# The first feature steps as a written list of single operations, up to step 28, and the second w_in block loaded ahead of x

## The chip, the cores and the metric

One NeuronCore of a Trainium2 chip runs the whole program. The metric is the device time of one execution in microseconds (us), and the figure given for a kernel is the median of its runs. Five engines work beside each other, each through its own queue in order: TensorE (PE in the profile, its weight loads are PEld), VectorE (DVE), ScalarE (ACT), GpSimd (POOL) and SyncE (SP), which here issues nearly all transfers (DMA). TensorE writes its results to PSUM, a memory of banks from which VectorE and ScalarE read them.

## The reference, cut to what matters

```python
# x [8,8,512,64], state [8,8,32,64], scale = 1/8
scores = scale * x @ state^T                 # [8,8,512,32]
a  = softmax(scores);   xread = a  @ state   # read by tokens
a2 = softmax(scale * state @ x^T); sread = a2 @ x   # read by slots
t  = concat([xread, sread], axis=2)          # 544 rows a batch, 4352 in all
t  = t.transpose(0,2,1,3).reshape(4352, 512)
# first block: w_in [512,2048], w_out [2048,512]
h = t @ w_in;  g = max(h, 0)**2;  t = g @ w_out
# second block: w_in [512,1024], g_ln [1024], w_out [1024,512]
h = t @ w_in;  s = h * softmax(h)
out = (s - mean(s)) / sqrt(var(s) + 1e-6) * g_ln @ w_out
```

The weight matrices reach the chip in 64-bit floats, and the kernel makes 32-bit numbers of them itself.

## The kernel before, in words

**Precision.** Every product that has to be exact is made of three matmuls. A number is split into a high part, which ScalarE writes by a copy to the matmul's format, and a low part, which VectorE writes by subtracting the high part. `triple` (lines 147 to 149) then adds high times high, high times low and low times high in one PSUM bank. Each of these matmuls has 512 columns.

**The tokens' read is never formed.** For a batch the product state @ w_in is made first (`ps_sw`, in 512-feature columns, called a chunk), and the hidden layer is the softmax `a` times that product. One **feature step** is one batch and 128 of the 2048 hidden features: six matmuls into `ps_h` (two contraction halves of three), ScalarE's relu and the square, the split of the square into `gh` (ScalarE) and `gl` (VectorE, line 830), and twelve matmuls `acc<-gh/gl,w1out` that add the step to four banks of output. There are 16 steps to a batch and 144 in all: eight batches, and a ninth block that holds all `sread` rows. The list `items` gives their order; the first 32 steps go chunk by chunk between batches 0 and 1, and steps 0 to 15 are their chunks 0 and 1.

**Weights are made ready beside that.** `convert_parts` turns a 128x512 block of 64-bit words into a high and a low part: on VectorE `cz`, `cu` twice, `ch`, `cz` and the low part (lines 215, 220, 221, 225, 231, 232), on ScalarE the exponent `cz` (line 216) between VectorE's first `cz` and its `ch`, and the high part (line 228) after `ch`. Sixteen blocks of w_in (`i0` to `if`, written to `w1i_d` and used for `ps_sw`) and sixteen of w_out (`o0` to `of`) go through it. `sw_part` makes `ps_sw` for two batches a call, ScalarE copies it to `ev_sw` (line 328) and it goes to DRAM (`sw_d`), from where `load_sw` fetches a batch's chunk into `stg` (line 406) and it is split again (`sw`).

**What sets the order.** The scheduler is switched off for four engines (`manual_schedule`): each engine runs its instructions in the order in which the code makes them. For the steps 0 to 15 this order is a written list, `PLAN`, of names such as `T02` (transpose x of batch 0, head pair 2), `i0` (the next piece of w_in block 0), `H00` (hidden of batch 0, feature 0), `G`, `L` (high, low), `P001` (one of four projections), `X0` (load x of batch 0), `I0`/`J0` (load the first or the second w_in block of a pair). A name mostly stands for several operations on several engines, made at once; `convert_parts` stops three times on its way. From step 16 on the loop `step` makes the instructions by rules: which step converts which block (`when`, `units`), where attention of the next batch comes in (`attention(b)`, a table of parts by step), where a chunk is loaded. At step 16 it issues three w_in fetches, a chunk load and the first two quarters of the next x (`load_xq`, line 485), at steps 17 and 18 the other two.

**The start.** `gcol` (the g_ln column, line 894) is fetched first on SP, then w_in block 0 (`I0`, line 878), the four parts of x of batch 0 (line 463), then w_in block 1 (`J0`) with blocks 2 and 3, and the four parts of x of batch 1. Batch 0's state comes on ScalarE's queue.

Of the kernel before, what the change touches and what calls it, by code (L numbers as in the profile page):

```python
# [20 lines left out]
def memory_attention_relu2_solu(  # L21
# [152 lines left out]

    def advance():

        for g in list(flying):
            if next(g, None) is None:
                flying.remove(g)
# [28 lines left out]
    def convert_parts(st, hi_r, lo_r, done=None):  # L208
# [26 lines left out]
        yield 1  # L235
# [3 lines left out]
    def convert_w1in(u, st):  # L239

        c, k = divmod(u, NM)

        t = u_tile("w1in")

        def done():
            nc.sync.dma_start(out=w1i_d[k][:, :, c * FC : (c + 1) * FC], in_=t.bitcast(F32))
            w1u[u] = t

        flying.append(convert_parts(st, t[:, 0, :], t[:, 1, :], done))

    w1o = []

    def convert_w1out(f, st):
        if f % 2 == 0:
            w1o.append(w_tile("w1out"))
        o = (f % 2) * 512
        flying.append(convert_parts(st, w1o[-1][:, 0, o : o + 512], w1o[-1][:, 1, o : o + 512]))
# [32 lines left out]
    def state_step(a, t):  # L290
# [9 lines left out]
        for i in range(2):  # L300
            if t == 0:
                split(bdw[0][:, i, :, i], bdw[0][:, i, :, 2 + i], v[:, :, :, :, i])
            else:
                o = bd[i][t]
                split(o[:, :, i], o[:, :, 1 - i], v[:, :, :, :, i])
# [4 lines left out]
    def sw_part(u, j):  # L310
# [6 lines left out]
        if at == 0:  # L317
            sw_ev[0] = evp.tile([P, 2, 512], F32, tag="ev", name="ev_sw")
        ev = sw_ev[0]
# [7 lines left out]
        triple(ps, [(lh, ll, t[:, 0, :], t[:, 1, :])], True, True)  # L327
        nc.scalar.activation(out=ev[:, at, :], in_=ps, func=AF.Copy)
        if single and j == 0:

            for b in range(2):
                if hp == 0:
# [8 lines left out]
        if j == 1:  # L341
            w1u.pop(u)

# [37 lines left out]
    def late_part(u, i):  # L381
        c, k = divmod(u, NM)
        if i == 0:
            sw_ev[0] = evp.tile([P, 2, 512], F32, tag="ev", name="ev_sw")
        ev = sw_ev[0]
# [33 lines left out]
    def split_sw(b, c):  # L419
        st = loading[b, c]  # L420
        loaded[b, c] = []
        for q in range(NQ):
            t = sw_tile("sw")
            split(t[:, 0, :], t[:, 1, :], st[:, q, :])
            loaded[b, c].append(t)
            if q == NQ - 1:
# [30 lines left out]
    def load_x(b):  # L457
        if b == 1:
            xs = wp.tile([P, NT, H, D], F32, tag="w", name="xs1")
        else:  # L460
            xs = xbuf.rearrange("p (t h d) -> p t h d", t=NT, h=H)
        for t in range(NT):
            nc.sync.dma_start(out=xs[:, t], in_=x[b].rearrange("h (p t) d -> t p h d", t=NT)[t])
        xs_t[b] = xs
# [25 lines left out]
    def attention(b):  # L490
# [5 lines left out]

        def trans_x(hp):
            if b >= 2:
                xt = atp.tile([P, S], F32, tag="st", name="xt", bufs=4)
                nc.vector.transpose(out=xt, in_=xq(hp))  # L500
                xh = xtp.tile([P, S], F32R, tag="xh", name="xh")
                xl = xtp.tile([P, S], F32R, tag="xl", name="xl")
                split(xh, xl, xt)
                v["xt", hp] = (xh, xl)
                return
            ps = ps_a.tile([P, 512], F32, tag=f"acc{hp}", name="ps_x")
            transposes(ps, [xs_t[b][:, t, 2 * hp : 2 * hp + 2].rearrange("p h d -> p (h d)") for t in range(NT)])
            if b == 0:
                xh = gp.tile([P, S], F32R, tag="gh", name="xh")
                xl = gp.tile([P, S], F32R, tag="gl", name="xl")  # L510
            else:

                if hp == 0:
                    new_a1()
                xh, xl = (a1_t[b][k][:, hp % 2, :] for k in range(2))
            v["rest", "x", hp] = split_bank(xh, xl, ps)
            v["xt", hp] = (xh, xl)

        def scores_t(hp):
            xh, xl = v.pop(("xt", hp))  # L520
# [3 lines left out]
            if b < 2:  # L524
                if i == 0:
                    v["ps", q] = bank("ps_s")
                lh, ll = (bdw[0][:, i, q, k : k + 2].rearrange("p l n b -> p (l n) b")[:, :, b] for k in (0, 2))
                triple(v["ps", q], [(lh, ll, xh, xl)], i == 0, i == 1)
                if i == 1:
                    nc.scalar.activation(out=v["st", q], in_=v["ps", q], func=AF.Copy)  # L530
                return
            ps = bank("ps_s")
            lt = bd[i][b // 2][:, q].rearrange("p l n b -> p (l n) b")[:, :, b % 2]
            nc.tensor.matmul(out=ps, lhsT=lt, rhs=xh, start=True, stop=False)
# [1010 lines left out]
```

## Time and profile before

| | |
|---|---|
| median of three runs | 1058.01 us (1054.23 to 1058.95) |
| profiled execution | 1060.5 us |
| its span (first to last instruction) | 1058.7 us |
| granted TensorE clock, mean | 0.994 |
| TensorE busy | 1027.7 us (97%) |
| VectorE busy | 783.9 us (74%) |
| ScalarE busy | 634.9 us (60%) |

A span is the time between the first and the last instruction of the trace; the execution's own time is 1.8 us more. A matmul's end in the trace is modelled and matmuls overlap, so TensorE's busy time says little about how densely they follow each other; the number of matmuls in a stretch (the x in the view of stretches) says more. The granted clock is 1.00 at 2.4 GHz and 0.50 at 1.2 GHz. A wait is put down to what released it last.

### The profile page before, as it was taken

Reading aid. Unit: us, or ns where it says so; the run is one execution under the profiler, and the core shown is the slowest. Engines: PE = TensorE matmul, PEld = TensorE weight load, DVE = VectorE, ACT = ScalarE, POOL = GpSimd, SP = SyncE. Lnnn points to the kernel's source line nnn. Section 1 sums busy time; section 2 is a strip of 40 time slices with the busy share of each in tenths; the row PEclk is TensorE's granted clock in tenths of the full one; section 3 lists DMA queues with packets and bytes.
Section 4 is the critical chain, followed back from the end, with each engine's and each line's share of the span. In section 5 each row is a group of like instructions: output and inputs, shape, how many; then the busy total and the mean of one; then the engine's idle time right before and its main releaser. Section 6 shows DMA issues by size and latency. Waiting matters only on the chain.

```text
span 1058.7 us, 14931 instructions
## 1 busy us (share of the span) xinstructions
PE 1027.7 (97%) x5142; PEld 847.0 (80%) x5142; DVE 783.9 (74%) x1373; ACT 634.9 (60%) x1063; POOL 138.9 (13%) x168
## 2 busy tenths in 40 slices
PE   5899998999999999999999999999999999999998
PEld 4688776888888888888888888897888888888877
DVE  6899979777677578588686554578977877877871
ACT  6899776556556565465464443465765665666562
POOL 1000000000000000000000022222232233234110
PEclk9899999999999999999999999999999999999999
DMA  9769798387388395452531413633544444444441
GB/s 253 263 234 301 263 237 238 123 224 210 124 235 227 124 262 169 99 146 89 130 90 56 144 60 115 204 105 115 194 145 163 166 139 150 167 162 142 143 133 50
DMA packets 182956, 174.54 MB, mean 165 GB/s; under 512 B 98784, under 2 KB 132832, under 8 KB 182880
## 3 DMA queue, kind: packets, MB, share of 16 engines
q1 hardware_dynamic: 182160, 173.33, 52.9%
q8 instruction: 40, 0.66, 0.2%
q10 hardware_dynamic: 720, 0.26, 0.1%
q14 instruction: 36, 0.29, 0.1%
HBM read 106.43 MB, written 66.06 MB: 163 GB/s over the span
## 4 chain that ended last, share of the span: by engine, by line
PE 80%; DVE 9%; DMA 5%; ACT 2%; issue 2%; SPq 1%; POOL 1%; DVEq 0%; ACTq 0%; POOLq 0%
PE b L975 14%; PE acc L147 10%; PE acc L149 10%; PE acc L148 10%; PE ps_h L147 5%; PE ps_o L1118 5%; PE ps_o L1116 5%; PE ps_o L1117 5%; PE ps_h L149 5%; PE ps_h L148 5%; DMA sw_d<-ev_sw 1%; PE ps_sr L613 1%; DVE ch L225 1%; DMA st64w<-in_moe_w_in_dram 1%; DMA stg<-sw_d 1%
## 5 line engine op out<-in xcount | busy, mean ns | idle before, releaser
L147 PE MATMUL acc<-gh,w1out 128*128 128x512 f32 (+1 forms) x576 | 219.6, 381 | 2.9 <-DVE ev_x L854 1.6
L149 PE MATMUL acc<-gh,w1out 128*128 128x512 f32 (+1 forms) x576 | 217.9, 378 | 0.0
L148 PE MATMUL acc<-gl,w1out 128*128 128x512 f32 (+1 forms) x576 | 217.8, 378 | 0.0
L811 ACT ACTIVATE r<-ps_h 128x512 f32<-128x512 f32 (+1 forms) x144 | 82.1, 570 | 123.3 <-PE ps_h L149 122.5
L830 DVE TENSOR_TENSOR gl<-r,gh 128x512 fp32r<-128x512 f32 (+1 forms) x144 | 96.7, 672 | 60.1 <-ACT gh L825 53.7
L147 PEld LDWEIGHTS acc<-gh,w1out 128*128 128x128 f32 x576 | 108.7, 189 | 24.4 <-DVE ev_x L854 2.8
L149 PEld LDWEIGHTS acc<-gh,w1out 128*128 128x128 f32 x576 | 108.6, 189 | 20.5
L815 DVE TENSOR_TENSOR r<-r,ps_h 128x512 f32<-128x512 f32 (+1 forms) x120 | 77.6, 647 | 63.7 <-ACT r L811 62.8
L148 PEld LDWEIGHTS acc<-gl,w1out 128*128 128x128 f32 x576 | 108.7, 189 | 19.9
L825 ACT ACTIVATE gh<-r 128x512 fp32r<-128x512 f32 (+1 forms) x120 | 72.1, 601 | 71.2 <-DVE r L815 71.2
L1118 PE MATMUL ps_o<-w,ll 128*128 128x512 f32 x272 | 106.3, 391 | 1.3 <-DVE ll L1097 1.0
L1116 PE MATMUL ps_o<-w,lh 128*128 128x512 f32 x272 | 106.2, 390 | 0.1
L1117 PE MATMUL ps_o<-w,lh 128*128 128x512 f32 x272 | 105.9, 389 | 0.0
L149 PE MATMUL ps_h<-ah,sw 128*128 128x512 f32 x256 | 100.9, 394 | 3.4 <-DVE sw L437 2.2
L147 PE MATMUL ps_h<-ah,sw 128*128 128x512 f32 x256 | 103.0, 402 | 0.0
L148 PE MATMUL ps_h<-al,sw 128*128 128x512 f32 x256 | 100.5, 393 | 0.0
L203 POOL TENSOR_TENSOR cw<-cw,ce 128x512 f32<-128x512 f32 x16 | 20.7, 1294 | 543.9 <-DVE ce L200 500.9
L975 PE MATMUL b<-w,x2h 128*128 128x512 f32 x272 | 84.1, 390 | 0.3 <-DVE hB L993 0.3
L1048 POOL TENSOR_TENSOR var<-var,mhalf 128x1 f32<-128x1 f32 x34 | 43.6, 1281 | 234.7 <-DVE var L1047 234.5
L1118 PEld LDWEIGHTS ps_o<-w,ll 128*128 128x128 f32 x272 | 51.0, 188 | 13.4 <-DVE ll L1097 2.7
L149 PEld LDWEIGHTS ps_h<-ah,sw 128*128 128x128 f32 x256 | 48.5, 189 | 14.7 <-DVE sw L437 2.6
L1027 ACT ACTIVATE e<-hA,nm 128x1024 f32<-128x1024 f32 x17 | 19.6, 1151 | 67.2 <-DVE nm L1022 67.2
(232 smaller groups left out, 2082.9 us busy)
## 6 DMA issues: line engine op xcount, KB each, us to landing
ln_d<-ln_sq SPq DMA_DIRECT2D x32, 512.0 KB, 3.2
ln_t<-ln_d SPq DMA_DIRECT2D x128, 128.0 KB, 2.8
stg<-sw_d SPq DMA_DIRECT2D x120, 128.0 KB, 3.1
sw_d<-ev_sw SPq DMA_DIRECT2D x28, 512.0 KB, 3.5
st<-in_moe_w_out_dram SPq DMA_DIRECT2D x24, 512.0 KB, 5.2
st_x<-x_d SPq DMA_DIRECT2D x34, 256.0 KB, 3.7
w1i_d<-w1in SPq DMA_DIRECT2D x16, 512.0 KB, 4.6
st<-in_moe_w_in_dram SPq DMA_DIRECT2D x16, 512.0 KB, 5.2
```

What stands on the lines that cost most here:

```text
L147: nc.tensor.matmul(out=ps, lhsT=lh, rhs=rh, start=first and i == 0, stop=False)
L148: nc.tensor.matmul(out=ps, lhsT=lh, rhs=rl, start=False, stop=False)
L149: nc.tensor.matmul(out=ps, lhsT=ll, rhs=rh, start=False, stop=last and i == n - 1)
L811: nc.scalar.activation(out=r, in_=ps, func=AF.Relu)
L815: nc.vector.tensor_tensor(out=r, in0=r, in1=ps, op=ALU.mult)
L825: nc.scalar.activation(out=gh, in_=r, func=AF.Copy)
L830: nc.vector.tensor_tensor(out=gl, in0=r, in1=gh.bitcast(F32), op=ALU.subtract)
L975: nc.tensor.matmul(out=ps, lhsT=l, rhs=r, start=first and k == 0 and j == 0, stop=k == 1 and j == 2, skip_group_check=True,)
L1048: nc.gpsimd.tensor_tensor(out=var, in0=var, in1=mhalf, op=ALU.pow)
L1116: nc.tensor.matmul(out=ps, lhsT=a, rhs=wt[:, 0, o : o + 512], start=(k == 0), stop=False)
L1117: nc.tensor.matmul(out=ps, lhsT=a, rhs=wt[:, 1, o : o + 512], start=False, stop=False)
L1118: nc.tensor.matmul(out=ps, lhsT=bb, rhs=wt[:, 0, o : o + 512], start=False, stop=(k == NK - 1))
```

## The change

The written list reaches to step 27 instead of step 15, and the loop takes over at step 28 (`steady`). Each function that the list calls stops (`yield`) after one operation or a few of one engine, so that a name stands once in the list for each of its stops, and operations of different names can be put between them: `i0` now stands nine times instead of three, `T02` and `H00` twice. The list is written anew from its first name on. New names fetch what the loop fetched before: `x` (earlier part of x2), `q` and `h` (quarters and halves of the next x), `y` (state of the late batches), `a` (parts of batch 2's attention), `g` (`gcol`). The rules for steps below 28 in the loop go. `J0` stands ahead of `X0`, and `gcol` is fetched later. The program issues the same instructions as before: 4888 on TensorE, 1341 on VectorE, 986 on ScalarE, 173 on GpSimd and 731 on SyncE, counted in the two built programs without the ones that only wait or set registers.

```diff
     def convert_parts(st, hi_r, lo_r, done=None):
...
         nc.vector.tensor_scalar(out=zu, in0=hi, scalar1=0x7FFFFE00, scalar2=None, op0=ALU.bitwise_and)
+        yield 1
         nc.scalar.activation(out=zi, in_=zi, func=AF.Relu, scale=8.0, bias=rebias)
-
+        yield 1
         u = cvp.tile([P, 512], F32, tag="cw", name="cu", bufs=4)
         uu = u.bitcast(U32)
         nc.vector.tensor_scalar(out=uu, in0=hi, scalar1=0x1FF, scalar2=None, op0=ALU.bitwise_and)
+        yield 1
         nc.vector.scalar_tensor_tensor(out=u, in0=lo, scalar=2.0**-32, in1=uu, op0=ALU.mult, op1=ALU.add)
         yield 1
...
         for t in range(NT):
             nc.sync.dma_start(out=xs[:, t], in_=x[b].rearrange("h (p t) d -> t p h d", t=NT)[t])
-        xs_t[b] = xs
+            yield 1
...
-        if not times:
-            nc.scalar.activation(out=gh, in_=r, func=AF.Square)
-            nc.scalar.activation(out=r, in_=r, func=AF.Square)
-        else:
-            nc.scalar.activation(out=gh, in_=r, func=AF.Copy)
+        nc.scalar.activation(out=gh, in_=r, func=AF.Copy if times else AF.Square)
         return b, f, n, r, gh
...
-    nc.sync.dma_start(out=gcol, in_=g_ln.rearrange("(k p) -> p k", p=P))
...
-    when = {("o", f): w for f, w in zip(range(12, NF), (20, 21, 22, 23))}
-    when |= {("i", u): w for u, w in zip(range(3 * AHEAD + 1, NU), (16, 17, 18))}
...
+    def hidden_part(b, f):
+        ps = hid_ps[b, f] = hidden(b, f, loaded[b, f // FPC], *a1_t[b], S)
+        yield 1
+        r, rest = square(ps, S, f >= 3 * FPC)
+        hid[b, f] = b, f, S, r, f >= 3 * FPC
+        if f >= 3 * FPC:
+            yield 1
+            rest()
+
+    def high_part(b, f):
+        sq[b, f] = high(*hid[b, f])
+        r, times = hid.pop((b, f))[3:]
+        if not times:
+            yield 1
+            nc.scalar.activation(out=r, in_=r, func=AF.Square)
+
+    def parts(k, a):
         if k in "TNSRQABCDEF":
-            att[a[0]][k](a[1])
+            yield from att[a[0]][k](a[1])
...
         elif k == "X":
-            load_x(a[0])
+            yield from load_x(a[0])
+        elif k == "g":
+            nc.sync.dma_start(out=gcol, in_=g_ln.rearrange("(k p) -> p k", p=P))
...
+        elif k == "x":
+            x2_part[a[0], a[1]] = fetch32(x2p_d[a[0]][:, 2 * a[1] : 2 * a[1] + 2, :])
+        elif k == "q":
+            load_xq(*a)
+        elif k == "h":
+            load_half(*a)
+        elif k == "y":
+            late_state(a[0])
+        elif k == "a":
+            att2[a[0]][a[1]][a[2]]()
+
+    def piece(p):
+        if p not in steps:
+            steps[p] = parts(p[0], [int(c, 16) for c in p[1:]])
+        next(steps[p], None)
 
     PLAN = """
-    I0 X0 J0 I2 i0 J2 X1 i0 U0 O0 O1 T02 T00 i0 i1 N02 T03 i2 N00 Z W00 S02 T01 N03 i2 N01 i1 i1 S00 i3 S03
...
+    I0 J0 i0 X0 i0 i0 i0 i1 X0 i1 i0 X0 U0 i1 i0 X0 I2 J2 i1 U0 T02 i1 i0 i1 O0 U0 T00 U0 T03 X1 X1 i1 X1
...
-        if s == 4 * FPC and chunks[5] not in loading:
-            load_sw(*chunks[5])
...
-            if s == 4 * FPC:
-                load_xq(w + 1, 0)
...
-    steady = range(4 * FPC, (B - 1) * NF)
+    steady = range(7 * FPC, (B - 1) * NF)
```

On SP, at the very start, the kernel before issues this (`st64w` is a raw w_in block, `xs` x of batch 0, `xs_234` x of batch 1):

```order
L894 DMA gcol<-in_moe_g_ln_dram 128x8x1
L878 DMA st64w<-in_moe_w_in_dram 128x1024
L463 DMA xs<-in_x_dram 128x8x64 x4
L878 DMA st64w<-in_moe_w_in_dram 128x1024 x3
L463 DMA xs_234<-in_x_dram 128x8x64 x4
L170 DMA st_251<-in_moe_w_out_dram 128x1024
```

And the changed kernel, in the same place of SP's queue:

```order
L893 DMA st64w<-in_moe_w_in_dram 128x1024 x2
L476 DMA xs<-in_x_dram 128x8x64 x4
L893 DMA st64w<-in_moe_w_in_dram 128x1024 x2
L170 DMA st_258<-in_moe_w_out_dram 128x1024
L476 DMA xs_272<-in_x_dram 128x8x64 x4
L170 DMA st_346<-in_moe_w_out_dram 128x1024
```

The second w_in block has moved ahead of the four parts of x, and `gcol` is gone from the head.

On VectorE, about step 17, the kernel before converts one w_in block (`st_1582`) from its first to its last operation without a break:

```order
L830 TENSOR_TENSOR gl<-r,gh 128x512
L215 TENSOR_SCALAR cz<-st_1582 128x512
L220 TENSOR_SCALAR cu<-st_1582 128x512
L221 SCALAR_TENSOR_TENSOR cu<-st_1582,cu 128x512
L225 SCALAR_TENSOR_TENSOR ch<-st_1582,cz 128x512
L231 TENSOR_SCALAR cz<-ch 128x512
L232 SCALAR_TENSOR_TENSOR w1in<-cu,cz 128x512
L651 STREAM_TRANSPOSE xt<-xs 128x512
L830 TENSOR_TENSOR gl<-r,gh 128x512
L437 TENSOR_TENSOR sw<-stg,sw 128x512
```

In the changed kernel two blocks (`st_1657` and `st_1643`) are under way at once about there, with other work between their operations:

```order
L219 TENSOR_SCALAR cz<-st_1657 128x512
L843 TENSOR_TENSOR gl<-r,gh 128x512
L239 SCALAR_TENSOR_TENSOR w1in<-cu,cz 128x512
L676 TENSOR_TENSOR xl<-xt,xh 128x512
L219 TENSOR_SCALAR cz<-st_1643 128x512
L699 TENSOR_TENSOR st<-ps_s,st 64x512
L225 TENSOR_SCALAR cu<-st_1657 128x512
L225 TENSOR_SCALAR cu<-st_1643 128x512
L227 SCALAR_TENSOR_TENSOR cu<-st_1657,cu 128x512
L231 SCALAR_TENSOR_TENSOR ch<-st_1657,cz 128x512
L227 SCALAR_TENSOR_TENSOR cu<-st_1643,cu 128x512
L231 SCALAR_TENSOR_TENSOR ch<-st_1643,cz 128x512
```

Between a block's `cz` and its `ch`, where ScalarE's `cz` has to be done, VectorE now has eight operations for the one block and six for the other, instead of two.

On SP, the kernel before issues the quarters of the next x (`xs`, line 485) in one stretch at steps 16 to 18:

```order
L170 DMA st_1580<-in_moe_w_in_dram 128x1024
L170 DMA st_1582<-in_moe_w_in_dram 128x1024
L170 DMA st_1584<-in_moe_w_in_dram 128x1024
L406 DMA stg<-sw_d_57 64x512
L406 DMA stg<-sw_d_58 64x512
L406 DMA stg<-sw_d_59 64x512
L406 DMA stg<-sw_d_60 64x512
L274 DMA st_1592<-x2p_d_117 128x1024
L485 DMA xs<-in_x_dram 32x16x32 x8
L246 DMA w1i_d_63<-w1in 256x1x512
L274 DMA st_1641<-x2p_d_117 128x1024
L485 DMA xs<-in_x_dram 32x16x32 x4
```

In the changed kernel the four quarters stand apart, the first 37 rows earlier in the queue; these are the second and the third:

```order
L170 DMA st_1222<-in_moe_w_out_dram 128x1024
L498 DMA xs<-in_x_dram 32x16x32 x4
L170 DMA st_1252<-in_moe_w_out_dram 128x1024
L353 DMA sw_d_57<-ev_sw 256x1x512
L170 DMA st_1291<-in_moe_w_out_dram 128x1024
L353 DMA sw_d_58<-ev_sw 256x1x512
L498 DMA xs<-in_x_dram 32x16x32 x4
L170 DMA st_1344<-in_moe_w_in_dram 128x1024
L353 DMA sw_d_60<-ev_sw 256x1x512
L353 DMA sw_d_59<-ev_sw 256x1x512
```

Each quarter now has w_out or w_in fetches right behind it in the queue.

## Rows read from the trace of the kernel before

**Rows 1.** The page: busy time of TensorE, VectorE and ScalarE over the span.

```profile
PE 1027.7 (97%) x5142; PEld 847.0 (80%) x5142; DVE 783.9 (74%) x1373; ACT 634.9 (60%) x1063; POOL 138.9 (13%) x168
```

**Rows 2.** Busy us and instructions by stretch, granted clock, DMA share, GB/s.

```profile
0.00:45.00 45.00, 28.87 (x119) 21.18 (x120) 33.38 (x66) 30.86 (x59) 4.06 (x12) 0.89 0.88 264
45.00:120.00 75.00, 74.93 (x456) 61.49 (x455) 72.11 (x147) 67.21 (x126) 0.00 (x0) 1.00 0.75 257
120.00:130.00 10.00, 8.78 (x39) 6.96 (x38) 9.20 (x20) 8.09 (x16) 0.00 (x0) 1.00 0.86 283
130.00:170.00 40.00, 36.70 (x155) 28.02 (x154) 32.42 (x58) 26.22 (x46) 0.00 (x0) 1.00 0.86 247
170.00:180.00 10.00, 7.84 (x28) 6.01 (x27) 9.64 (x19) 6.81 (x13) 0.00 (x0) 0.83 0.93 251
220.00:260.00 40.00, 40.00 (x178) 33.11 (x177) 31.71 (x54) 23.64 (x43) 2.60 (x2) 1.00 0.78 223
```

**Rows 3.** Waits of TensorE from 120 to 180 us: total, times, longest.

```profile
PE ps_h L149 <- DVE sw L437: 2.2, 1, 2.2
PE acc L147 <- DVE ev_x L854: 1.6, 2, 1.4
PE ps_h L149 <- DVE sw L123: 1.2, 1, 1.2
```

**Rows 4.** Waits of VectorE from 128 to 190 us.

```profile
DVE gl L830 <- ACT r L823: 3.2, 4, 1.4
DVE ch L225 <- ACT cz L216: 1.7, 1, 1.7
DVE cz L215 <- DMA st<-in_moe_w_out_dram: 1.0, 1, 1.0
DVE ev_x L854 <- DMA sw_d<-ev_sw: 0.6, 1, 0.6
DVE xt L651 <- DMA xs<-in_x_dram: 0.4, 1, 0.4
```

**Rows 5.** The stretch at the lower clock near 176 us, as Rows 2.

```profile
175.20:178.30 3.10, 3.10 (x9) 2.42 (x8) 3.00 (x7) 1.65 (x3) 0.00 (x0) 0.50 0.83 234
```

**Rows 6.** The chain of waits from 128.9 to 173.3 us, shares by line.

```profile
by line: DMA sw_d<-ev_sw 29.3%; DMA xs<-in_x_dram 16.1%; DMA stg<-sw_d 14.9%; SPq L470 8.1%; issue 5.7%; ACT ev_sw L328 5.7%; ACT xh L655 2.8%; ACT gh L822 2.4%; DVE ev_x L854 1.9%; DVE cu L221 1.6%; DVE gl L830 1.5%; ACT w1in L228 1.4%; DV
```

**Rows 7.** VectorE's instructions from 5 to 14 us; in brackets idle before, releaser.

```profile
5.76 0.43 DVE L215 TENSOR_SCALAR cz<-st64w 128x512 uint32<-128x512 uint32 x1 [4.37 <-DMA st64w<-in_moe_w_in_dram]
...
9.77 0.42 DVE L123 TENSOR_TENSOR bdw<-ps_st,bdw 128x256 fp32r<-128x256 f32 x1 [1.92 <-ACT bdw L122]
10.65 0.42 DVE L123 TENSOR_TENSOR bdw<-ps_st,bdw 128x256 fp32r<-128x256 f32 x1 [0.45 <-ACT bdw L122]
...
13.17 0.43 DVE L215 TENSOR_SCALAR cz<-st64w 128x512 uint32<-128x512 uint32 x1 [1.03 <-DMA st64w<-in_moe_w_in_dram]
```

**Rows 8.** SP's issues from 0 to 17 us: start, us until issued, what.

```profile
0.74 0.45 SPq L894 DMA_DIRECT2D gcol<-in_moe_g_ln_dram  x1
1.25 0.56 SPq L878 DMA_DIRECT2D st64w<-in_moe_w_in_dram  x1
1.85 4.86 SPq L463 DMA_DIRECT2D xs<-in_x_dram  x4
6.76 2.04 SPq L878 DMA_DIRECT2D st64w<-in_moe_w_in_dram  x3
```

**Rows 9.** Waits of TensorE from 0 to 45 us, the four longest.

```profile
PE ps_st L296 <- DMA a_st<-in_state_dram: 8.2, 1, 8.2
PE ps_x L130 <- ACT ah L127: 1.8, 2, 1.0
PE ps_s L148 <- ACT xl L131: 1.6, 1, 1.6
PE ps_a L138 <- DVE e L575: 1.3, 1, 1.3
```

**Rows 10.** Waits in SP's queue from 120 to 190 us, the longest.

```profile
SPq L406 <- DVE sw L437: 7.2, 1, 7.2
```

More of the change, by code (lines that the diff above doesn't have):

```diff
@@ L173, in memory_attention_relu2_solu, with run @@
     flying = []
+    def run(g):
+        for _ in g:
+            pass
     def advance():
@@ L495, in new_a1, with a1 @@
             a1_t[b] = tuple(a1p.tile([P, NQ, S], F32R, tag=t, name=t) for t in ("ah", "al"))
-        def trans_x(hp):
[L498 to L505, printed above, removed]
+        def a1():
+            if b not in a1_t:
+                new_a1()
+            return a1_t[b]
@@ L506, in trans_x, with low_in_bank @@
+        def low_in_bank(hi, lo, ps):
+            nc.tensor.matmul(out=ps, lhsT=negi, rhs=hi, start=False, stop=True, skip_group_check=True)
+            yield 1
+            nc.scalar.activation(out=lo, in_=ps, func=AF.Copy)
+        def trans_x(hp):
             ps = ps_a.tile([P, 512], F32, tag=f"acc{hp}", name="ps_x")
             transposes(ps, [xs_t[b][:, t, 2 * hp : 2 * hp + 2].rearrange("p h d -> p (h d)") for t in range(NT)])
+            yield 1
             if b == 0:
                 xh = gp.tile([P, S], F32R, tag="gh", name="xh")
+            else:
+                xh = a1()[0][:, hp % 2, :]
+            v["px", hp], v["xh", hp] = ps, xh
+            nc.scalar.activation(out=xh, in_=ps, func=AF.Copy)
@@ L510, in trans_x, with low_x @@
+        def low_x(hp):
+            ps, xh = v["px", hp], v["xh", hp]
+            nc.tensor.matmul(out=ps, lhsT=negi, rhs=xh, start=False, stop=True, skip_group_check=True)
+            yield 1
+            if b == 0:
                 xl = gp.tile([P, S], F32R, tag="gl", name="xl")
             else:
[L513 to L517, printed above, removed]
@@ L519, in scores_t, with scores @@
[L519 to L520 removed]
+                xl = a1()[1][:, hp % 2, :]
+            v["xl", hp] = xl
+            nc.scalar.activation(out=xl, in_=ps, func=AF.Copy)
+        def scores(hp):
+            xh, xl = v["xh", hp], v["xl", hp]
             q, i = hp // 2, hp % 2
             if i == 0:
[L523 to L540 removed]
@@ L601, in sread @@
         def sread(half):
-            if half == 0:
+            if "ps_sr" not in v:
                 v["ps_sr"] = bank("ps_sr")
@@ L1289, in step @@
         w, ws = divmod(s, NF)
-        for kind, u in [unit for w_ in ((s, s + 1, s + 2) if s == 4 * FPC else (s + 2,)) for unit in units.get(w_, [])]:
-            if (kind, u) not in raw:
-                (fetch_w1in if kind == "i" else fetch_w1out)(u)
-        for unit in units.get(s, []):
-            begin(*unit)
         g = s - 2 * NF
@@ L1336, in step @@
             att.extend(attention(w + 1))
-        sw = next((u for k, u in units.get(s - 2, []) if k == "i"), None)
         last = high(*squares.pop(0)) if squares else None
@@ L1351, in step @@
         split_d.clear()
-        r, rest = square(ps, n, s >= 24)
+        r, rest = square(ps, n, True)
         for part in after:
             part()
-        q = s % FPC - (2 if 20 <= s < 24 else 1)
+        q = s % FPC - 1
         if s // FPC + 1 < len(chunks) and q in (0, 1):
@@ L1369, in step @@
         for m in range(4):
-            if s < 24 and m > 0:
-                advance()
-            if sw is not None and m < 2:
-                sw_part(sw, m)
             if late is not None and m > 1:
@@ L1376, in step @@
             if job:
-                project(*job, m)
-        if s == 5 * FPC or s % FPC == 3 and s > 5 * FPC:
-            i = s // FPC + (1 if s == 5 * FPC else 2)
+                run(project(*job, m))
+        if s % FPC == 3:
+            i = s // FPC + 2
             if i < len(chunks) and chunks[i][0] < B and chunks[i] not in loading and chunks[i] not in loaded:
@@ L1502, in memory_attention_relu2_solu @@
     for m in range(4):
-        project(*pend[1], m)
+        run(project(*pend[1], m))
     sb.close()
```

230 lines of the change are left out of this document (125 added, 105 removed).

## The prediction, as it stood before the run

> **What bounds the kernel now.** I read the page first, then the view of stretches, then the waits of TensorE and of VectorE, and last the chain of waits and SP's queue where the stretches showed a loss. The page says TensorE 97% busy over the span [rows 1]; that hides where it is thin, because a matmul's end is modelled. The stretches show it. From 220 to 260 us TensorE issues 178 instructions in 40 us, so a slot in dense running is 40/178 = 0.2247 us [rows 2]. Nearly all instructions there and from 120 to 180 us are 512-column matmuls, so counts can be compared. From 120 to 180 us there are 39 + 155 + 28 = 222 instructions [rows 2]; dense they take 222 x 0.2247 = 49.9 us, and 10.1 us of the 60 are lost. The start loses more: 119 instructions in the first 45 us are 26.7 us of work, so 18.3 us are lost, 8.2 of them before the first matmul, which waits for the state [rows 2, 9]. From 45 to 120 us TensorE is busy for 74.93 of 75 us, and from 220 us on it is full [rows 2]. So the change can win in two places only, the start and the steps that the loop used to order, about 16 to 24; both lie in what is written anew.
>
> In the second place TensorE's three longest waits, 5.0 us together, all end by VectorE [rows 3]. VectorE is busy 72.11 of 75 us from 45 to 120, yet from 130 to 170 only 32.42 of 40: it idles 7.6 us just before TensorE starves, and is full again (9.64 of 10) once TensorE is behind [rows 2]. That idle time is what has to be looked at. Of it 3.2 us wait for ScalarE's second square ahead of `gl` and 1.7 us for the exponent ahead of `ch`, 4.9 us in all; 2.0 us wait for transfers (1.0, 0.6 and 0.4) [rows 4]. After the longest of TensorE's waits its clock stands at 0.50, the 1.2 GHz level, for about 3.1 us [rows 5].
>
> **The change part by part.** The engines get the same instructions in the same number, so nothing is added or removed; each term is about a wait.
>
> *Steps 16 to 27 in the list.* Between a block's `cz` and its `ch` VectorE now has six or eight operations instead of two, and the block's exponent on ScalarE runs beside them; `gl` stands apart from the square in the same way. I let VectorE's idle time go but for the 2.0 us that transfers end: 7.6 - 2.0 = 5.6 us. If TensorE isn't starved, the stretch at 1.2 GHz goes as well, which gives back half of 3.1, 1.6 us. Together 7.2 us. What is late next is VectorE itself: its work from 120 to 180 us is 9.20 + 32.42 + 9.64 = 51.3 us [rows 2], so these 60 us cannot shrink by more than 8.7 unless VectorE comes to them earlier. The bounds are 0 (the waits only change their names) and 10.1 us (all that TensorE loses there).
>
> *The start.* VectorE has its first block at 5.76 us; then it idles 1.92 + 0.45 + 1.03 = 3.4 us until it has the second block at 13.17 [rows 7], which SP issued at 6.76, behind the four parts of x [rows 8]. Now the second block goes out right behind the first, and the first half a microsecond earlier, since `gcol` took 0.74 to 1.25 of the queue [rows 8]. At best VectorE gains 3.4 + 0.5 = 3.9 us. At worst x is late by the whole second block: 0.52 MB at the 264 GB/s of the first 45 us [rows 2] is 2.0 us, and TensorE's first transposes of x, right behind the state's, would show all of it. VectorE's work feeds TensorE only later in the start, where TensorE waits longer for ScalarE (1.8 and 1.6 us) than for it (1.3) [rows 9]. I take the row nearest to it, the 1.03 us that the second block itself ends: a gain of 1.0 us.
>
> The Trainium skill speaks against this edit: in "DMA: Bandwidth & Descriptors", under "Queues, rings and completion order", it says that each DMA engine consumes descriptors in ring order, so that the second block would pass wholly ahead of x. By that rule the start would be at its bad end and the sum would be -7.2 + 2.0 = -5.2 us; no row here shows in which order the bytes of the two came.
>
> *Steps 0 to 15 made anew.* From 45 to 120 us TensorE has nothing to gain. VectorE's 96% there is the cover for every operation that is moved; its idle 2.9 us could double, so the bounds are 0 and +2.9 us. I take 0. *`gcol` later, and step 28 on:* 0.45 us of SP's time somewhere after 17 us, beside TensorE's work, from 0 to +0.45; the loop from step 28 on has the same order, and where TensorE is full [rows 2], it only starts earlier. I take 0 for both.
>
> The sum is -7.2 - 1.0 = -8.2 us. It is made against the profiled execution, 1060.5 us (span 1058.7 and 1.8 around it), and gives 1052.3. That execution is 2.5 us above the median of the three runs, so against 1058.0 I forecast **1049.8 us**. The ends of the terms add to -14.0 and +5.4, that is 1044.0 and 1063.4.
>
> **The rivals.**
>
> *Transfers hold the stretch.* Of the chain from 128.9 to 173.3 us, 29.3 + 16.1 + 14.9 = 60.3%, 26.8 of 44.4 us, are transfers [rows 6], and the DMA share of 120 to 180 us is 0.87 on average [rows 2]: 52.3 us of transfer. At the highest share of these rows, 0.93, they need 56.3 us, so the stretch shrinks by 3.7 and not 7.2, and with the start's 1.0 the time is 1053.3. For it speak the chain and that the same bytes have to move. Against it, the DMA share from 45 to 120 us is 0.75 [rows 2], which leaves 18.7 us free, and the new queue sends the first quarter of x there.
>
> *Everything goes.* VectorE's 3.4 us of the start reach TensorE and all 10.1 us are won: 1058.0 - 13.5 = 1044.5. For it speaks that VectorE was nearly full from 45 to 120 us, so what it gains before stays gained; against it that TensorE at the start waits longer for the state and for ScalarE than for VectorE [rows 9].
>
> *The list moves the waits and wins nothing.* 1058. For it: the full TensorE of 45 to 120 us is the work of an older list in coarser pieces, and says little of this one. Against it: it is also a written order and leaves no idle time there.
>
> *Slower: a quarter of x holds SP's queue.* The loads of the next x may go only when the matmuls that read batch 0's x are done, and each quarter now has w_out or w_in fetches right behind it, which VectorE's list wants at a fixed place. If SP stands there, VectorE stands later, and all behind it in its queue. The longest hold in the queue of before is 7.2 us [rows 10]. Two of four quarters with such a hold are 14.4 us, against 8.2 won: 1064.2. It decides from holds of 8.2 us in all. Against it: with the quarters apart, each has had more time for its buffer to come free. The Trainium skill, in "DMA: Bandwidth & Descriptors", "Anatomy of one DMA", says that DMA engines do not wait on semaphores and that the wait happens on the issuing sequencer before dispatch; the one piece of 7.2 us agrees, and by that rule the rival's 1064.2 is open.
>
> **How the numbers follow.** Forecast 0.46, with 1045.5 to 1053.5 as its own range; transfers hold 0.24; everything goes 0.12; nothing won 0.07; slower 0.11. About 0.5%, 5.3 us, is what a measurement of this kernel can tell from no change, so faster means under 1052.7. Faster takes 0.42 of the forecast, 0.07 of the transfers and the 0.12: 0.61. Slower is 0.10, the part of the last case over 1063.3. The rest, 0.29, is the same. From 1043.5 to 1061 leaves out the slower case and little else.
>
> **What would show it.** Right: from 110 to 170 us in the new profile VectorE over 95% busy, TensorE with about 44 instructions per 10 us, no stretch at 0.50 there, and `gl` without waits for ScalarE; VectorE's second block well before 10 us; the same picture as before from step 28 on, earlier by the gain. Wrong: VectorE idle behind transfers in that stretch, SP's quarters with holds of several microseconds, x landing later with TensorE's first transposes after 11 us, or new waits of TensorE from 45 to 120 us.

## The result, and the profile after

The changed kernel takes 1047.91 us (median of 4 runs, 1047.27 to 1049.80) against 1057.16 us of the kernel before in the same comparison (4 runs, 1054.23 to 1058.95): a ratio of 0.9918, with a 95% interval of 0.9891 to 0.9945. Run again later in this study, beside 17 runs of the kernel before (1058.13 us), it took 1048.61 us (5 runs, 1048.06 to 1050.64), a ratio of 0.9914 (0.9898 to 0.9930). So 9 us are won. The forecast was 1049.8. The profiled execution took 1049.8 us, its span 1048.0; before it was 1060.5.

The busy line of the page after, beside [rows 1]:

```profile
PE 1022.6 (98%) x5142; PEld 845.0 (81%) x5142; DVE 778.4 (74%) x1373; ACT 633.2 (60%) x1063; POOL 138.2 (13%) x168
```

The same instructions run; only TensorE's modelled time is 5 us shorter. Where the time came from stands in the view of stretches after (columns as in [rows 2]: length, then busy us and count of TensorE, weight loads, VectorE, ScalarE and GpSimd, the granted clock, DMA share, GB/s):

```profile
0.00:45.00 45.00, 28.78 (x130) 21.00 (x131) 34.42 (x71) 31.98 (x61) 4.06 (x12) 0.96 0.88 247
45.00:120.00 75.00, 75.00 (x453) 61.57 (x452) 69.29 (x145) 67.13 (x128) 0.00 (x0) 1.00 0.82 262
120.00:130.00 10.00, 10.00 (x46) 8.28 (x45) 9.79 (x20) 7.50 (x16) 0.00 (x0) 1.00 0.87 295
130.00:170.00 40.00, 40.00 (x178) 32.99 (x177) 37.59 (x74) 31.32 (x58) 0.00 (x0) 1.00 0.82 240
170.00:180.00 10.00, 10.00 (x45) 7.95 (x43) 8.77 (x18) 6.46 (x12) 0.00 (x0) 1.00 0.81 192
180.00:220.00 40.00, 39.86 (x237) 32.76 (x237) 30.14 (x52) 20.00 (x36) 1.30 (x1) 1.00 0.84 243
```

From 120 to 180 us TensorE issues 46 + 178 + 45 = 269 instructions instead of 222. At 0.2247 us each that is 60.4 us, so nothing is lost there any more, where 10.1 us were lost before. The clock stays at 1.00 through this stretch, and the view of TensorE's waits is empty from 45 to 180 us, where before it had the three of [rows 3] and two shorter ones (1.1 and 0.5 us). VectorE, whose idle time stood beside TensorE's, is busy 9.79 + 37.59 + 8.77 = 56.2 of the 60 us instead of 51.3. Its waits from 128 to 190 us, beside [rows 4]:

```profile
DVE r L832 <- ACT r L828: 1.1, 1, 1.1
DVE cz L219 <- DMA st<-in_moe_w_in_dram: 0.8, 1, 0.8
...
DVE cz L219 <- DMA st<-in_moe_w_out_dram: 0.5, 1, 0.5
DVE gl L843 <- ACT r L1239: 0.4, 1, 0.4
```

The 3.2 us of `gl` are 0.4, and the 1.7 us of `ch` are gone.

The start has 130 instructions in 45 us, 29.2 us of work, so 15.8 us are lost instead of 18.3. Part of that is the clock. The stretch of the start at 0.50, the 1.2 GHz level, is 10 us long before and 3.3 us after; in the 5 us before it fell, TensorE was busy for 2.65 and 2.11 us (first before, then after):

```profile
31.60:41.60 10.00, 8.20 (x24) 5.90 (x24) 9.06 (x20) 6.49 (x13) 0.00 (x0) 0.50 0.65 215
```

```profile
37.10:40.40 3.30, 3.22 (x10) 2.04 (x9) 3.00 (x7) 2.86 (x6) 0.00 (x0) 0.50 0.85 318
```

TensorE's waits there, beside [rows 9]:

```profile
PE ps_st L303 <- DMA a_st<-in_state_dram: 8.7, 1, 8.7
PE ps_s L147 <- ACT st L552: 2.7, 1, 2.7
PE ps_x L533 <- ACT ah L529: 1.9, 2, 1.2
```

The wait of 2.7 us is new. VectorE at the start, beside [rows 7] (start, us, engine, line, operation; idle before and releaser in brackets):

```profile
4.65 0.43 DVE L219 TENSOR_SCALAR cz<-st64w 128x512 uint32<-128x512 uint32 x1 [3.25 <-DMA st64w<-in_moe_w_in_dram]
...
6.24 0.43 DVE L219 TENSOR_SCALAR cz<-st64w 128x512 uint32<-128x512 uint32 x1
...
10.28 0.42 DVE L315 TENSOR_TENSOR bdw<-ps_st,bdw 128x256 fp32r<-128x256 f32 x1 [1.01 <-ACT bdw L313]
```

The second block is begun at 6.24 us instead of 13.17. And SP's queue, which the experiments showed to matter, first in the kernel before and then after: its issues of the next x from 78 to 150 us (start, us until all were issued, what, how many).

```profile
132.14 7.77 SPq L485 DMA_DIRECT2D xs<-in_x_dram  x8
...
```

```profile
78.01 2.04 SPq L498 DMA_DIRECT2D xs<-in_x_dram  x3
...
91.49 2.64 SPq L498 DMA_DIRECT2D xs<-in_x_dram  x4
...
99.58 3.72 SPq L498 DMA_DIRECT2D xs<-in_x_dram  x4
...
129.65 2.02 SPq L498 DMA_DIRECT2D xs<-in_x_dram  x4
```

Before, two quarters hold the queue for 7.77 us within the stretch in which TensorE starves; after, three quarters have been issued by 103.3 us, each by itself (the first issue of the first quarter lies ahead of 78 us).

### The profile page after: what moved, and what is told of

It reads as the page before. It is cut to its first block, busy times and chain, and to the rows that moved or that the text cites. A ratio compares the mean times of both kernels' runs of the same rounds, so it can differ in the third digit from the quotient of the medians.

```text
span 1048.0 us, 14967 instructions
## 1 busy us (share of the span) xinstructions
PE 1022.6 (98%) x5142; PEld 845.0 (81%) x5142; DVE 778.4 (74%) x1373; ACT 633.2 (60%) x1063; POOL 138.2 (13%) x168
## 4 chain that ended last, share of the span: by engine, by line
PE 89%; DMA 4%; DVE 2%; ACT 2%; SPq 1%; issue 1%; POOL 1%; DVEq 0%; ACTq 0%; POOLq 0%
PE b L986 14%; PE acc L147 11%; PE acc L149 11%; PE acc L148 11%; PE ps_h L147 6%; PE ps_h L149 6%; PE ps_h L148 6%; PE ps_o L1129 5%; PE ps_o L1128 5%; PE ps_o L1127 5%; PE ps_sr L628 2%; DMA st_x<-x_d 1%; PE ps_c L558 1%; PE ps_sw L147 1%; PE ps_sw L399 1%
## 5 line engine op out<-in xcount | busy, mean ns | idle before, releaser
L838 ACT ACTIVATE gh<-r 128x512 fp32r<-128x512 f32 (+1 forms) x144 | 87.1, 605 | 72.2 <-DVE r L832 70.0
L1127 PEld LDWEIGHTS ps_o<-w,lh 128*128 128x128 f32 x272 | 51.1, 188 | 11.0 <-ACT lh L1102 0.6
```

The source lines that it names most:

```text
L838: nc.scalar.activation(out=gh, in_=r, func=AF.Copy if times else AF.Square)
L1127: nc.tensor.matmul(out=ps, lhsT=a, rhs=wt[:, 0, o : o + 512], start=(k == 0), stop=False)
```

## The experiments

The prediction explained the second place by single operations on VectorE. First the old start was put back by itself, then the two orders were taken apart: the written steps 16 to 27 without the new list ahead of them, and the new list without them.

**The old start.** SP's first names as in the kernel before:

```diff
-    I0 J0 i0 X0 i0 i0 i0 i1 X0 i1 i0 X0 U0 i1 i0 X0 I2 J2 ...
+    g0 I0 X0 X0 X0 X0 J0 i0 i0 i0 i0 i1 i1 i0 U0 i1 i0 I2 J2 ...
```

> The changed kernel with SP's old start: the g_ln column first, then the first w_in block, the four parts of x, and only then the second block. The order on TensorE, VectorE and ScalarE stays that of the changed kernel. If the 2.5 us won in the first 45 us come from this order of the queue, the changed kernel's 130 TensorE instructions from 0 to 45 us fall to 119 to 122, VectorE's second block starts after 12 us, and the time rises by 1.5 to 2.5 us to about 1050. If they come from the new order of the list instead, the counts and the time stay within 0.5 us of the changed kernel's 1047.9.

It took 1051.48 us (6 runs, 1049.20 to 1053.37): by the medians 3.6 us of the gain go, or 2.9 against the changed kernel's second time, more than expected; single runs of the two kernels overlap. The count to 45 us (129) isn't the 119 to 122 that was expected. But the 130 of the changed kernel's profile, from which that was reckoned, are few: the six other profiles of kernels that start like it, but for at most one name, have 138 to 145. Beside them the old start costs 9 to 16 instructions, 2.0 to 3.6 us of work. The new wait below stands in the place of the 2.7 us for `st`, which are absent in this execution. VectorE starts the second block at 11.92 us. ScalarE's timeline shows what follows:

```profile
12.38 0.72 ACT L221 ACTIVATE cz<-cz,rebias 128x512 int32<-128x512 int32 x1 [4.94 <-DVE cz L219]
...
15.60 1.57 ACT L529 ACTIVATE xh<-ps_x 128x512 fp32r<-128x512 f32 x3
```

In the new list the second block's exponent (at 12.38 us here) stands on ScalarE ahead of x's high copies. If the block comes late, these start at 15.60 instead of 11.02 us, and TensorE waits for them, 4.0 us at once.

**The old list, with the written steps 16 to 27 behind it.** Steps 0 to 15 and the start in the order of the kernel before on every engine (its `i0` stands for four names of the new list, and so on), then the 264 names that are left, in the new order:

```diff
-    I0 J0 i0 X0 i0 i0 i0 i1 X0 ... P160 q21 i9 ... H04 q20 O8 ... a020 ...
+    g0 I0 X0 X0 X0 X0 J0 I2 i0 i0 i0 i0 ... P053 q21 q20 a020 q23 a110 l12 ...
```

> Steps 0 to 15 and the start in the order of the kernel before, on all four engines and SP; steps 16 to 27 written out as in the changed kernel. Theory (the written order of steps 16 to 27 alone wins the second place): from 120 to 180 us TensorE issues 260 or more instructions instead of 222, no half-clock stretch near 176 us, the start is that of before (119 to 45 us), and the time is 1049 to 1051. Rival (VectorE has to come to these steps earlier, thanks to the new list of steps 0 to 15): 225 to 245 instructions from 120 to 180 us and 1053 to 1056.

Neither: 1060.84 us (12 runs; ratio to before 1.0033, 1.0019 to 1.0047), slower than the kernel before. TensorE's longest wait from 120 to 180 us, and its chain of waits there (start, us, what):

```profile
PE ps_h L147 <- ACT r L828: 6.1, 1, 6.1
```

```profile
130.94 0.50 SPq L414
131.49 2.68 DMA stg<-sw_d
134.29 0.49 issue
...
136.05 0.50 ACT r L828
136.59 0.79 PE ps_h L147
```

Without the old steps between them, three quarters of x are issued in one go, 12 issues from 124.07 to 130.90 us. The chunk load (L414) stands behind them, ScalarE's split of that chunk behind the load, and the relu for which TensorE waits behind that.

**The new list, with the old loop behind it.** The mirror image: only the names of the steps 0 to 15, in the new order, then the rules of the kernel before from step 16 on.

```diff
-    steady = range(7 * FPC, (B - 1) * NF)
+    steady = range(4 * FPC, (B - 1) * NF)
...
+            if s == 4 * FPC:
+                load_xq(w + 1, 0)
```

> Start and steps 0 to 15 in the order of the changed kernel, steps 16 to 27 by the rules of the kernel before, whole conversions in their three pieces. Theory: the start keeps its 130 instructions to 45 us, but 120 to 180 us loses its 8 to 10 us again with a half-clock stretch; 1054 to 1056. Rival (the new list brings VectorE earlier, and that is what fills 120 to 180 us): at most 4 us lost there, 1049 to 1051.

Slower than before again: 1060.34 us (12 runs; ratio 1.0034, 1.0019 to 1.0048). The start is no worse than after (145 instructions), but TensorE waits once for 6.5 us (`ps_sw` for `ev_sw`), and the chain of waits leads there from SP's issues of x and their landing (start, us, what):

```profile
132.96 0.24 PE ps_sw L149
133.20 0.28 SPq L498
...
134.68 4.79 DMA xs<-in_x_dram
...
140.88 0.60 DVE sw L449
```

VectorE's longest wait there is one that the prediction's theory names, for the exponent:

```profile
DVE ch L231 <- ACT cz L221: 4.2, 1, 4.2
```

ScalarE runs that exponent behind its copy of the chunk, which waits 4.5 us for the chunk's load, so both theories have a part in this run.

So the halves do not add: each alone costs 3.0 to 3.5 us by the medians (1057.30 us for the kernel beside them), both together win 9. But each half also takes the quarters of x from their places, since three of them (`q21`, `q20`, `q23`) stand among the names of steps 0 to 15 in the new list. In both the chain passes SP's issues of x (L498) ahead of TensorE's longest wait. That gave a second theory, SP's queue, which the next four runs set against the first.

**Whole blocks.** The changed kernel, with the operations of each of seven blocks in a row at the place of its first name:

```diff
-    ... id P062 ... id P071 id V12 Ke id q22 id P073 ...
+    ... id id id id id id id id id P062 ... P071 V12 Ke q22 P073 ...
```

> The changed kernel, but each of the seven blocks that only steps 16 to 27 convert (id, ie, if, oc to of) has all its operations in a row, at the place of its first. Theory of the prediction (single operations, spread out on VectorE and ScalarE, take the idle time away): VectorE waits 4 us or more for the exponents and the high parts from 120 to 190 us, TensorE loses 3 to 7 us there, 1051 to 1055. New theory (the order and spacing of the transfers on SP's queue do it): within 2 us of the changed kernel's 1047.9, with no TensorE wait over 1 us from 120 to 180 us.

1061.94 us (9 runs; ratio to before 1.0036, 1.0023 to 1.0048): all of the gain goes and 4 us more. From 120 to 180 us the waits of TensorE, then those of VectorE, are:

```profile
PE ps_sw L147 <- ACT ev_sw L340: 4.8, 2, 2.8
PE ps_sw L147 <- DVE st L699: 2.6, 1, 2.6
PE acc L148 <- DVE gl L843: 1.1, 1, 1.1
```

```profile
DVE cz L219 <- DMA st<-in_moe_w_in_dram: 5.6, 1, 5.6
DVE ch L231 <- ACT cz L221: 3.8, 1, 3.8
```

This looks like a proof that the spread is needed, but the edit changes SP's queue as well. The last name of a w_in block is its store to `w1i_d`. Moved forward with the rest, it stands in SP's queue before VectorE is done with the block, and SP waits for it, 6.9 us at the longest (in the changed kernel 2.1). SP's waits from 95 to 185 us, and the chain from there (start, us, what):

```profile
SPq L253 <- DVE w1in L239: 15.6, 4, 6.9
```

```profile
129.72 0.51 SPq L253
130.29 0.60 SPq L170
130.94 6.66 DMA x2p_d<-ev_x
```

The fetch for which VectorE waits 5.6 us is issued behind that store, and so is the store of `ev_x`, for which ScalarE waits 4.6 us and, behind it, TensorE 2.8 us; the chain from there runs on to TensorE's 2.6 us for `st`. Only the 3.8 us for the exponent, and TensorE's second wait for `ev_sw` behind them (4.8 - 2.8 = 2.0 us), are plainly the effect of whole blocks. How much of the 14.0 us the spread is worth isn't shown by this run.

**The quarters together.** The changed kernel with all four quarters of x ahead of their first use; VectorE's and ScalarE's order is untouched:

```diff
-    ... i9 q21 i9 ... H04 q20 O8 ... a020 W91 Wa0 q23 ... id q22 id ...
+    ... i9 i9 ... H04 O8 ... q21 q20 q23 q22 a020 W91 Wa0 ... id id ...
```

> The changed kernel, but the four quarters of the next x (q21, q20, q23, q22) stand side by side on SP's queue, just ahead of the first use of them (a020). New theory (SP's queue): sixteen issues of 0.5 us each hold the queue for 8 us or more, the fetches and stores behind them are late, and TensorE waits again somewhere from 105 to 140 us: 3 to 8 us lost, 1051 to 1056. Theory of the prediction (single operations): nothing on VectorE or ScalarE is moved, within 1 us of 1047.9.

1056.67 us (10 runs; ratio to before 0.9986, 0.9971 to 1.0000): 8.8 us lost by SP's order alone. The queue, ScalarE's longest wait, and TensorE's:

```profile
94.41 12.35 SPq L498 DMA_DIRECT2D xs<-in_x_dram  x16
106.86 0.52 SPq L353 DMA_DIRECT2D sw_d<-ev_sw  x1
```

```profile
ACT ev_sw L340 <- DMA sw_d<-ev_sw: 9.0, 1, 9.0
```

```profile
PE ps_c L558 <- ACT ev_sw L340: 5.5, 1, 5.5
```

A store of `ev_sw` stands behind the sixteen issues, which hold the queue for 12.35 us; ScalarE needs the buffer that it empties, and TensorE a bank that ScalarE empties. TensorE is all but still from 105 to 110 us, at a DMA share of 0.68 (columns as in the stretches):

```profile
105.00:110.00 5.00, 0.49 (x1) 0.19 (x1) 2.44 (x5) 0.00 (x0) 0.00 (x0) 0.76 0.68 165
```

So the order on SP is needed, and this run moves nothing else.

**The quarters apart in the kernel before.** Three of four quarters issued in its written list; all else as before:

```diff
+    ... F01 q20 ... H04 q21 ... H05 q22 ...
...
-            if s == 4 * FPC:
-                load_xq(w + 1, 0)
-            if ws in (0, 1, 2):
+            if ws in (0, 1, 2) and s not in (4 * FPC, 4 * FPC + 1):
```

> The kernel before with three of the four quarters of the next x taken out of steps 16 and 17 and issued apart from each other in its written list, after F01, H04 and H05; all else, the whole conversions too, as before. New theory (SP's queue): the stretch of eight quarter issues at 132 to 140 us goes, TensorE issues 240 or more instructions from 120 to 180 us instead of 222, and 4 to 9 us are won: 1048 to 1053. Theory of the prediction (single operations): 222 to 230 instructions there, 1056 to 1058.

1058.35 us (10 runs; ratio 0.9998, 0.9982 to 1.0014): nothing, where the second theory expected 4 to 9 us. It falls here as the only cause. The issues now lie at 91, 103 and 108 us, and TensorE issues 40 + 162 + 37 = 239 instructions from 120 to 180 us in the profiled execution instead of 222, but its waits there are still on VectorE:

```profile
PE ps_h L149 <- DVE sw L437: 2.1, 1, 2.1
PE ps_h L149 <- DVE sw L123: 1.1, 1, 1.1
```

**The old list with quarters apart, and the written steps 16 to 27.** The second experiment, with the three quarters at those places of the old list.

```diff
-    ... F01 ... H04 ... H05 ... P053 q21 q20 a020 q23 a110 ...
+    ... F01 q20 ... H04 q21 ... H05 q22 ... P053 a020 q23 a110 ...
```

> The old order of the start and of steps 0 to 15 with the written steps 16 to 27 (1060.8 us so far), and with three quarters of the next x issued apart in the old part, after F01, H04 and H05. New theory (SP's queue): the 6.1 us wait of TensorE at 130 to 137 us goes, and the time falls by 7 to 10 us to 1051 to 1054. Rival (VectorE comes too late to step 16 from the old list): TensorE still waits 4 us or more there, over 1056.

1054.71 us (8 runs, 1054.17 to 1055.52; ratio 0.9971, 0.9957 to 0.9985): 6.1 us better than without, a little short of what was expected. What is left from 120 to 180 us is shorter:

```profile
PE ps_h L147 <- ACT r L828: 2.0, 1, 2.0
PE ps_h L149 <- DVE sw L435: 1.5, 1, 1.5
```

This run and the one before it have the same start, the same list up to step 15 and three quarters at the same places; they differ in the steps 16 to 27, by rules there and written here. So with the quarters apart the written steps are worth 1058.35 - 1054.71 = 3.6 us, where with the quarters in one go (the second experiment) they cost 3.5. Of the remaining 6.8 us to the changed kernel 2.9 to 3.6 are the old start, by its own run; the rest, 3 to 4 us, is by subtraction the new list of steps 0 to 15. Through what it wins them wasn't tested.

| | us | against the changed kernel's 1047.9 |
|---|---|---|
| start taken back | 1051.48 | +3.6 |
| seven blocks whole, stores on SP earlier too | 1061.94 | +14.0 |
| quarters of x together | 1056.67 | +8.8 |
| list of steps 0 to 15 and start taken back, quarters apart | 1054.71 | +6.8 |
| **alone in the kernel before** | | **against 1058.1** |
| new start | 1058.02 | -0.1 |
| quarters apart | 1058.35 | +0.2 |

Two more runs took the start apart. **The g_ln column first:**

```diff
-    I0 J0 i0 X0 ... i3 g0 R00 ...
+    g0 I0 J0 i0 X0 ... i3 R00 ...
```

> The changed kernel with the g_ln column first on SP's queue again, and the second w_in block still ahead of x. Splits the two edits of the start, which together are worth 3.6 us in the changed kernel's list (1051.5 with the old start). If the second block's place is what counts, 1047.9 to 1048.9 (the column's 0.44 us of the queue and no more); if the column does, 1050 or more.

1048.16 us (4 runs, 1047.29 to 1048.55): the column's place is worth nothing, so the 2.9 to 3.6 us are the second block's. **The new start in the kernel before:**

```diff
-    I0 X0 J0 I2 ... Z W00 ...
+    I0 J0 X0 I2 ... Z g0 W00 ...
```

> The kernel before with only the new start of SP's queue: second w_in block ahead of x, g_ln column behind the state of the later batches; its list of steps as it was. Theory of the prediction (the edit is worth something by itself, VectorE gets its second block earlier): 0.5 to 2 us under the kernel before. Rival (only a list that converts the second block before x's high copies makes use of it): within 0.5 us of the kernel before, or up to 2 us slower because x lands later.

1058.02 us (12 runs; ratio 0.9997, 0.9986 to 1.0007): nothing. The rival holds; VectorE's rows show why:

```profile
10.20 0.42 DVE L123 TENSOR_TENSOR bdw<-ps_st,bdw 128x256 fp32r<-128x256 f32 x1 [3.23 <-ACT bdw L122]
...
12.48 0.42 DVE L215 TENSOR_SCALAR cz<-st64w 128x512 uint32<-128x512 uint32 x1
```

The block is there, but in the old list `bdw` stands ahead of it, and VectorE idles 3.23 us for that. The granted clock tells the lists apart too. Its mean over the first 45 us is 0.89 to 0.92 in all five profiles with the old list of steps 0 to 15, this one with the new start included, and 0.96 to 1.00 in all nine with the new list, the one with the old start included.

Last, the wait of 2.7 us that was new in the start. In the profile after, ScalarE holds at its copy of the first chunk (`sw<-stg`) for 2.8 us until the chunk's transfer lands, and the scores' copy `st` (L552) is queued behind. **The scores' copy first:**

```diff
-    ... U1 V00 J4 Q00 Q00 o1 N13 S11 V10 ...
+    ... U1 S11 V00 J4 Q00 Q00 o1 N13 V10 ...
```

> The changed kernel with one name moved: ScalarE's copy of the scores (st, the second S11) stands ahead of its copy of the first chunk (sw from stg, V00), which waits 2.8 us for a transfer at 34.7 us and holds the copy behind it. Theory: TensorE's wait of 2.7 us for st at 33 to 36 us goes, 1.5 to 2.7 us are won, 1045.2 to 1046.4. Rival: TensorE then waits for the same transfer one step later, or VectorE, which is nearly full from 45 us on, gives the gain back: within 0.5 us of 1047.9.

1047.08 us (6 runs, 1045.30 to 1051.36). The wait is gone from its profile (142 instructions to 45 us), but the runs don't separate it from the changed kernel. One reason is that the wait isn't always there: **the changed kernel once more**,

> The changed kernel itself once more, beside the others of this chip: 1047 to 1049, whichever theory holds. If it comes out above 1051, differences of 2 to 4 us between the earlier runs can't be read as effects of the edits.

at 1048.61 us, also has 142 instructions to 45 us in its profile, and no such wait. The loads of the first chunks landed after 4.8 us there (median) and after 6.6 in the first profile, so how late they land differs between executions of the same kernel. **With the state of the later batches fetched earlier as well:**

```diff
-    ... O1 I6 o0 S03 S01 Z o0 ...
+    ... O1 Z I6 o0 S03 S01 o0 ...
```

> The kernel with ScalarE's copy of the scores ahead of its copy of the first chunk, and besides it the state of the later batches fetched ahead of a w_in block (Z ahead of I6). That kernel's profile shows TensorE waiting 1.45 us for this state at 26 us and 0.6 us for the chunk's transfer. Theory (TensorE's own waits at the start set the time, since it is full from 37 us on): 0.5 to 1.5 us under the kernel with the first move alone, 1045.5 to 1046.5. Rival (VectorE and ScalarE, each busy over 90% from 24 to 45 us, set it): no difference, 1047 or more.

1046.14 us (4 runs, 1045.60 to 1046.91; ratio to before 0.9886, 0.9871 to 0.9901), the fastest kernel of this study. Each of its runs is faster than each of the changed kernel beside it (1048.06 to 1050.64), and the medians differ by 2.5 us. From the kernel with the first move alone it isn't separated by the runs (1045.30 to 1051.36). Its start, beside the first row of the stretches after:

```profile
0.00:45.00 45.00, 31.27 (x148) 23.45 (x148) 38.12 (x78) 35.62 (x68) 4.07 (x12) 1.00 0.95 278
```

148 instructions are 33.3 us of work: 11.7 us are lost, against 15.8 and, in the second profile of the changed kernel, 13.1.

## Why the prediction was right, and where it wasn't

**The places.** That the change can win only at the start and from 120 to 180 us held: TensorE is full in between (75.00 of 75 us), as before. Of the signs for the second place the clock held, at 1.00; VectorE, busy 56.39 of the 60 us from 110 to 170 (94%), came a little short of the 95%.

**Steps 16 to 27, forecast -7.2.** In the profiled pair the whole 10.1 us went, the upper bound. The step that was mis-sized is "I let VectorE's idle time go but for the 2.0 us that transfers end". Transfers end 1.3 us of VectorE's waits after (0.8 + 0.5), and none of it reaches TensorE. The sum also set idle time of 130 to 170 us against waits of 128 to 190 us; the rows name 6.9 of its 7.6 us. The bound "cannot shrink by more than 8.7 unless VectorE comes to them earlier" was passed, but not in the way that it names. Up to 120 us VectorE has done less work than before, 103.7 us instead of 105.5, and from 180 to 220 us more, 30.14 us instead of the 28.23 of this row of the kernel before:

```profile
180.00:220.00 40.00, 40.00 (x239) 32.92 (x238) 28.23 (x53) 20.86 (x39) 0.00 (x0) 1.00 0.50 140
```

Some of its work came later. The cause was at most half of the truth. SP's order is needed (8.8 us without it), and this the forecast gave to the rivals. The written steps 16 to 27 are worth 3.6 us where the quarters stand apart, and less than nothing where they don't. That it is the single operations in them that count was argued and not shown, since the run with whole blocks moves SP's stores too.

**The start, forecast -1.0.** Right in sign, too small (2.5 us by the profiled pair; 3.6 us, or 2.9, by the runs with the old start), and wrong in its reason. The row it rested on, VectorE's 1.03 us for the second block, isn't worth anything by itself: with the block there in time the old list gains 0.1 us. The gain belongs to block and list together. It also left out the clock. In the 10 us at 0.50 before, TensorE is busy 8.20 us; half of that, 4.1 us, is an estimate, by the prediction's own halving, of what the low level cost, against 1.6 us of 3.22 after. The long stretch at the low level goes with the old list of steps 0 to 15, and for the new one the forecast took 0. The Trainium skill ("DMA: Bandwidth & Descriptors", "Queues, rings and completion order") says that on each DMA engine descriptors are consumed in ring order. The 2.0 us that the prediction drew from it, x late by a whole block, did not show: SP began to issue x at 1.64 us instead of 1.85, its loads landed after 6.2 us (median) instead of 5.8, and the first transposes of x start at 9.55 us, against 9.04 before, both 0.88 us behind the first of the state's, which come 0.5 us later.

**Steps 0 to 15, forecast 0.** From 45 to 120 us it is 0, as forecast. As a term of a sum it was the wrong question: the old list and the old start, with all the rest of the change, cost 6.8 us, of which the start's own run explains 2.9 to 3.6. The working as a whole added edits that only work together.

**`gcol` and step 28 on, forecast 0.** The column is 0 by its own run. Behind step 28 a little is given back: 10.1 + 2.5 = 12.6 us are won up to 180 us, and the executions differ by 10.7. One wait of 1.0 us (`ps_s` for `ev_sw`, line 401) between 180 and 640 us is new; the rest wasn't followed up. So the sum came within 2 us of the median partly by luck, by errors that in part cancel: 2.9 and 1.5 us too little won, 1.9 given back.

**The rivals.** "Transfers hold the stretch" had the right place and argued the right counterpoint, that the first quarter of x goes out earlier; its price, from the DMA share, missed the point: the run with the quarters together loses 8.8 us by SP's order, and TensorE stands still in it at a DMA share of 0.68. "A quarter of x holds SP's queue" had the mechanism and the wrong kernel: it is the kernel before that issues eight in one stretch, and the change that ends it. The experiment with the quarters together shows that mechanism at work in the changed kernel, with one hold of 12.35 us instead of two of 7.2; 1056.67 us is still no slower than before. The Trainium skill ("DMA: Bandwidth & Descriptors", "Anatomy of one DMA") says that a semaphore wait happens on the issuing sequencer. The 6.9 us in which SP stands for VectorE in the run with whole blocks agree. Of the 12.35 us, sixteen issues at 0.49 us are 7.8 and a wait for TensorE's `acc` is 0.5; the view of waits names nothing for the rest.

**What wasn't settled.** Why each half alone is slower than before, rather than equal, was seen in its waits but not tested apart. What the spread of single operations is worth by itself stays open: whole blocks with the stores left at their places on SP were not run. Nor was it tested which operations of steps 0 to 15 keep the clock of the start up.

## What to carry to other kernels

When VectorE is over 90% busy next to a full TensorE, the order on every queue that feeds them, SP's included, is one condition and not a sum of edits: a part of a new schedule tried alone can be worth nothing or less. Read SP's rows for stretches of many small issues, and ask what stands behind them in its queue, before blaming the engine that waits. Read them in a test run too: an edit that is to move one engine's operations can move stores and fetches with them, as that of the whole blocks did. An earlier transfer pays only if the consumer's list uses it earlier.

## What the runs showed of the hardware

- SP's time for issuing is a resource. In the run with the quarters together, one of a quarter's four DMAs (32x16x32) takes 0.49 us of SP (median), all sixteen took 12.35 us, and what stands behind them in the queue was issued only then. The DMA share in the stretch where TensorE then starved, 105 to 110 us, was 0.68, so the DMA engines were not full there; from 95 to 100 us, while x was being issued, it was 1.05. The Trainium skill ("DMA: Bandwidth & Descriptors", "Issuing engines are not separate DMA queues") calls the time to initiate a DMA usually small relative to the DMA itself. Here one of these DMAs took 3.2 us to land (median), so that is so for one, and not for sixteen in a row.
- The landing of transfers at the start differs between executions of one kernel. The loads of the first chunks took 6.6 us in one profile of the changed kernel and 4.8 in the other (medians); TensorE waited 2.7 us behind them in the first and not in the second, and its count to 45 us is 130 and 142, a difference of 2.7 us of work.
